# A fused attention and two-MLP kernel: due times shifted by twenty drawn tables, a warm-up of TensorE, tanh for SiLU in one chunk, and four smaller edits

## The chip, the cores and the metric

The kernel runs on one core of a Trainium2 chip. The metric is the device time of one execution, in microseconds (us); three runs of the kernel before gave 1001.65, 1002.58 and 1002.89, median 1002.58. Engines: PE is TensorE (matmuls), DVE is VectorE, ACT is ScalarE, POOL is GpSimd, and SP issues nearly all DMAs. Each engine works through its own list of instructions in a fixed order; semaphores tie the lists together.

## The reference

Three steps in a row, in float32. Attention with random features over 4 batches, 8 heads, 576 tokens and head size 64: `phi(x) = exp(proj - |x|^2/2 - max) / sqrt(128)` with `proj = x omega^T` and 128 features, then `num = phi(q) (phi(k)^T v)` and `den = phi(q) sum(phi(k)) + 1e-6`, and their quotient. The heads side by side make 2304 rows of 512 columns. Then two MLPs:

```
x = (silu(x @ w_gate) * (x @ w_val)) @ w_out      # 512 -> 1536 -> 512
x = ((x @ w_a) * (x @ w_b)) @ w_out2
```

## The kernel before, in words

All of it is one launch with the tokens along the free axis. The 2304 tokens are cut into five chunks of 512, 512, 256, 512 and 512 (`spans`). For each chunk, queries and keys of a pair of heads go through `features` (a projection on PE, its maximum on DVE, exponentials on ACT), and `own` or `shared` makes the attention output. Chunks 0, 1 and 2 then run `layer(c, m)` for m = 0 (SiLU) and m = 1 (no activation); the last two chunks are taken as a pair (`pair(m, ...)`). A matrix product in float32 is made of three products of rounded parts: every operand is split into a high part (a copy rounded to the engine's format, by ACT) and a low part (the difference, by DVE or POOL), and PE does high*high, high*low and low*high (L936 to L938 in `layer`). In a pair, blocks of 2x2 are multiplied by seven products instead of eight (`seven`, with the sums and differences of the blocks made by DVE and POOL in L1016; all its matmuls are L994); only the last third of the down projection of m = 0 is done with eight (`plain`).

In `layer`, an up block f makes two PSUM banks, gate and value; ACT takes SiLU of the first (L954), DVE multiplies by the second (L957), and the result is split (L960 and L478). The exponentials (L632) and SiLU need different activation tables, and ACT loads one when it changes between them (ACT_TABLE_LOAD). Weights come as 64-bit words in chunk 0 and, half of them, in chunk 1: two ACT and two DVE instructions (L896 to L905) make floats of them; they are kept in DRAM and loaded again later.

No order is written out by hand. Every operation is given to a planner (`Plan.add`) with its engine, a cost, what it reads and writes, and a due time. `Plan.order` plays the engines forward: an engine that is free takes, of the operations whose inputs are there by its costs, the one with the smallest due time; buffers of a ring are handed out in the order in which they were recorded. The order that results is the program. So a shift of due times moves instructions everywhere, and on all engines.

Places that the change touches: `constants` (L503 on: omega, the table warm-up, the identity that POOL makes), `loads` and `keys` (the transposed keys of the first pair of heads, one DMA of 288 KB), `layer` (L954 to L957), `mixes` (splits and differences that the pair needs at its start), `seven`, `down` and `plain` (the pair's products), and `issue`.

Of the kernel before, what the change touches and what calls it, by code (L numbers as in the profile page):

```python
# [96 lines left out]
class Plan:  # L97
# [14 lines left out]
    RATE = 0.24  # L112
    HELD = {DVE: (1.0, 0.05), POOL: (1.0, 0.12)}
# [28 lines left out]

# [121 lines left out]
    def issue(self):  # L264
        for o in self.order():
            o.fn()
# [3 lines left out]
def attention_moe_moe(ctx: ExitStack, tc: tile.TileContext, qT, kT, q, k, v, omegaT,  # L270
# [192 lines left out]
    def pe(t):  # L463
        return dict(pace=t, lat=t + 0.17)
# [23 lines left out]
    AHEAD = 20.0  # L488

# [13 lines left out]
    def constants():  # L503
# [29 lines left out]
    def features(rT, tok, nt, step, f, due, length, how, psum, first):  # L533
# [39 lines left out]
        for g in range(0, nt, size):  # L573
# [25 lines left out]
            else:  # L599
                ps = psum.buf()  # L600
                for i in range(n):
                    def proj(i=i, ps=ps, g=g):
# [10 lines left out]
                       [(rT, *rT.state), (bd, *bd.state)], writes=[(ps, i)])  # L613
# [24 lines left out]
    def loads(rT, src, p, due, pieces):  # L638

        for b, a, z, to in pieces:  # L640
            on(SP, dma((z - a) / 2), due - 9, lambda b=b, a=a, z=z, to=to: nc.sync.dma_start(
                out=rT.tile[:, to:to + z - a], in_=src[b, p][:, a:z]), writes=[(rT, b)])
# [3 lines left out]
    def keys(b, p, due, length, how):  # L646

        rT, tok, vt = r_xT.buf(), r_kt.buf(), r_vt.buf()
        loads(rT, kT, p, due, [(b, 0, S, 0)])
# [275 lines left out]
    def layer(c, m):  # L925
# [16 lines left out]
        for f in range(NF):  # L942
# [4 lines left out]
            for g in range(2):  # L947
# [6 lines left out]
            on(ACT, act(n, 0, True), due, lambda a=a, ps=ps: nc.scalar.activation(  # L954
                out=a.tile[:, 0:n], in_=ps[0].tile[:, 0:n], func=AF.Silu if m == 0 else AF.Copy),
                reads=[(ps[0],)], writes=[(a,)], table="silu" if m == 0 else None)
            on(DVE, dve(n), due, lambda a=a, h=h, ps=ps: nc.vector.tensor_tensor(  # L957
                out=h.tile[:, 0:n], in0=a.tile[:, 0:n], in1=ps[1].tile[:, 0:n], op=ALU.mult),
                reads=[(a,), (ps[1],)], writes=[(h,)])
# [59 lines left out]
    def mixes(m, due, eng):  # L1019
# [6 lines left out]
        def keep(name, k, b):  # L1026
            hi, lo = r_cx.buf(), r_cx.buf()
            got[name, k] = (hi, lo)
            split(of(b), of(hi), of(lo), due)

        def first(k):
            keep("a11", k, x[0, k])
            s3 = r_tmp.buf()
            combine(eng[k], of(x[0, k]), of(x[1, k]), of(s3), ALU.subtract, due)
            keep("s3", k, s3)
            less.append(s3)
# [51 lines left out]
    def pair(m, eng):  # L1088
# [23 lines left out]
        def seven(w, x, late, read):  # L1112


            b0, b1, b2 = (ps_m.buf() for _ in range(3))
            b4, b3 = (b2, b1) if late else (b1, b2)
# [5 lines left out]
            for i, name in enumerate(order):  # L1122
                b, wn, xn, first, last = steps[name]
                product(b, w[wn], x[xn], now(6 * i), first, last)
                read(name, b)

        def up(f, late):
# [18 lines left out]
            seven(w, x, late, read)  # L1146
# [9 lines left out]
        def down(g, d, hx):  # L1156

            w = mixed_weights(m, 2 * NF + ND * d + g, 2 * NF + ND * (d + KD // 2) + g, now(), d == 0)
            e = now(42) - 15
# [5 lines left out]
            seven(w, hx, d == 0, read)  # L1165

        def plain(g, d, hx, more):
# [4 lines left out]
            for t, names in ((1, ("a21", "a22")), (0, ("a11", "a12"))):  # L1172
                for x, o in zip(i, (d, d + KD // 2)):
                    b = ps_m.buf()
                    hi, lo = parts_of[c, m, x]
                    for k, name in enumerate(names):
                        product(b, [(hi, lo, slice((2 * k + e) * P, (2 * k + e + 1) * P))
                                    for e in range(2)], hx[name], now(more), k == 0, k == 1)
                        more += 6
                    gain(b, (t, o), now(more) - 15)  # L1180
# [43 lines left out]
        for f, out in steps:  # L1224
# [6 lines left out]
            else:  # L1231
                down(*out, hx[out[0]])
                done += n_down // (KD // 2)
        for (t, d), o in sorted(acc.items()):
# [80 lines left out]
```

## Time and profile before

| | |
|---|---|
| median of 3 runs | 1002.58 us (1001.65 to 1002.89) |
| profiled execution | 1005.29 us |
| its span, first to last instruction | 1003.5 us |
| PE busy | 984.2 us, 98% of the span |
| DVE busy | 894.3 us, 89% |
| ACT busy | 725.3 us, 72% |
| POOL busy | 258.2 us, 26% |
| granted TensorE clock, mean | 0.998 |

The profiled execution lies 1.8 us above its own span and 2.7 us above the median of the runs. [...] Waits are listed by who waited and who ended the wait.

### The profile page before, as it was taken

How to read it: one execution, taken by the hardware profiler on the slowest of the kernel's cores; microseconds unless marked ns; L12 is line 12 of the kernel's file. 1: busy time of each engine (PE TensorE's matmuls, PEld its weight loads, DVE VectorE, ACT ScalarE, POOL GpSimd, SP SyncE). 2: the span in 40 equal slices, each digit the busy share in tenths (PEclk: the TensorE clock that was granted, in tenths of full speed). 3: DMA queues.
4: the chain of work that ended last, by engine and by line, in shares of the span. 5: the costliest groups of instructions: out<-in, count | busy, mean ns of one | idle time of the engine just before them, and what ended most of it. 6: DMA issues, size and time to landing. Idle time of an engine off the chain costs nothing.

```text
span 1003.5 us, 15362 instructions
## 1 busy us (share of the span) xinstructions
PE 984.2 (98%) x5144; PEld 829.3 (83%) x5144; DVE 894.3 (89%) x1593; ACT 725.3 (72%) x1523; POOL 258.2 (26%) x207
## 2 busy tenths in 40 slices
PE   7999999999999999999999999999999999999998
PEld 6878888878878888888888999988888887888886
DVE  5999889999968889998978879989889788989997
ACT  5978878798789898879868978666574645556351
POOL 1220023413502333454356424112020021202020
PEclk9999999999999999999999999999999999999999
DMA  8778776686876567665654555511212301121212
GB/s 250 238 258 243 229 244 200 217 252 189 286 227 197 176 190 241 203 188 166 192 165 131 147 160 172 171 61 33 74 43 63 95 22 53 32 74 42 61 35 84
DMA packets 92400, 153.12 MB, mean 153 GB/s; under 512 B 8736, under 2 KB 41120, under 8 KB 92320
## 3 DMA queue, kind: packets, MB, share of 16 engines
q1 hardware_dynamic: 92240, 152.11, 49.3%
q8 instruction: 40, 0.66, 0.3%
q14 instruction: 40, 0.33, 0.1%
q10 hardware_dynamic: 80, 0.03, 0.0%
HBM read 128.52 MB, written 23.59 MB: 152 GB/s over the span
## 4 chain that ended last, share of the span: by engine, by line
PE 78%; DVE 9%; ACT 6%; DMA 3%; issue 2%; POOL 1%; SPq 0%; DVEq 0%; ACTq 0%; POOLq 0%
PE ps_m L994 12%; PE ps_m L936 12%; PE ps_m L937 11%; PE ps_m L938 11%; PE ps_t L994 8%; PE ps_p L994 8%; PE ps_kv L994 4%; PE ps_kv L663 3%; PE ps_p L583 2%; DMA w64a<-w 1%; PE ps_t L869 1%; DVE wl L478 1%; PE ps_p L609 1%; PE ps_t L854 1%; DVE w L905 1%
## 5 line engine op out<-in xcount | busy, mean ns | idle before, releaser
L478 DVE TENSOR_TENSOR wl<-w,wh 128x512 fp32r<-128x512 f32 x254 | 190.8, 761 | 10.2 <-ACT wh L917 9.6
L936 PE MATMUL ps_m<-xh,wh 128*128 128x512 f32 (+1 forms) x504 | 189.2, 375 | 3.2 <-ACT a L954 2.5
L937 PE MATMUL ps_m<-xl,wh 128*128 128x512 f32 (+1 forms) x504 | 184.7, 366 | 0.7 <-DVE xl L478 0.7
L938 PE MATMUL ps_m<-xh,wl 128*128 128x512 f32 (+1 forms) x504 | 184.5, 366 | 0.7 <-DVE wl L478 0.7
L917 ACT ACTIVATE wh<-w 128x512 fp32r<-128x512 f32 x220 | 135.9, 632 | 32.1 <-DVE w L905 18.6
L478 POOL TENSOR_TENSOR rs<-xT,rs 64x576 fp32r<-64x576 f32 (+4 forms) x48 | 67.9, 1414 | 201.4 <-ACT rs L566 114.6
L936 PEld LDWEIGHTS ps_m<-xh,wh 128*128 128x128 f32 x504 | 95.9, 190 | 18.2 <-ACT a L954 3.8
L938 PEld LDWEIGHTS ps_m<-xh,wl 128*128 128x128 f32 x504 | 95.6, 190 | 16.8 <-DVE wl L478 1.2
L937 PEld LDWEIGHTS ps_m<-xl,wh 128*128 128x128 f32 x504 | 95.9, 190 | 13.7 <-DVE xl L478 1.3
L936 PE MATMUL ps_m<-hh,wh 128*128 128x512 f32 (+1 forms) x240 | 90.9, 379 | 0.0
L937 PE MATMUL ps_m<-hl,wh 128*128 128x512 f32 (+1 forms) x240 | 88.6, 369 | 0.0
L938 PE MATMUL ps_m<-hh,wl 128*128 128x512 f32 (+1 forms) x240 | 88.6, 369 | 0.0
L905 DVE SCALAR_TENSOR_TENSOR w<-w,w64a 128x512 uint32<-128x512 uint32 x90 | 69.9, 780 | 5.3 <-ACT w L896 5.2
L902 DVE SCALAR_TENSOR_TENSOR w64a<-w64a 128x512 uint32<-128x512 uint32 x90 | 69.0, 772 | 3.0 <-ACT w64a L899 2.9
L899 ACT ACTIVATE w64a<-w64a 128x512 uint32<-128x512 uint32 x90 | 60.9, 681 | 13.4 <-DMA w64a<-w 12.9
L896 ACT ACTIVATE w<-w64a 128x512 f32<-128x512 f32 x90 | 60.1, 675 | 0.6 <-DVE wl L478 0.6
L478 DVE TENSOR_TENSOR hl<-h,hh 128x512 fp32r<-128x512 f32 (+1 forms) x72 | 51.9, 722 | 1.6 <-ACT hh L960 1.4
L938 PEld LDWEIGHTS ps_m<-hh,wl 128*128 128x128 f32 x240 | 45.2, 189 | 8.0
L936 PEld LDWEIGHTS ps_m<-hh,wh 128*128 128x128 f32 x240 | 45.3, 189 | 7.6 <-issue 1.7
L960 ACT ACTIVATE hh<-h 128x512 fp32r<-128x512 f32 (+1 forms) x72 | 40.3, 561 | 15.3 <-DVE h L957 15.1
L937 PEld LDWEIGHTS ps_m<-hl,wh 128*128 128x128 f32 x240 | 45.4, 189 | 5.9
L825 POOL TENSOR_TENSOR xt<-qf,fT 128x512 f32<-128x512 f32 (+2 forms) x31 | 35.3, 1140 | 49.9 <-ACT qf L632 26.7
(850 smaller groups left out, 2635.4 us busy)
## 6 DMA issues: line engine op xcount, KB each, us to landing
w64a<-w SPq DMA_DIRECT2D x90, 512.0 KB, 4.3
w<-kept SPq DMA_DIRECT2D x180, 256.0 KB, 2.7
kept<-w SPq DMA_DIRECT2D x72, 256.0 KB, 5.0
w64b<-w SPq DMA_DIRECT2D x18, 512.0 KB, 4.7
kt<-k_t SPq DMA_DIRECT2D x16, 320.0 KB, 3.8
vt<-v_t SPq DMA_DIRECT2D x16, 320.0 KB, 4.4
xT<-kT SPq DMA_DIRECT2D x16, 288.0 KB, 3.8
qt<-q_t SPq DMA_DIRECT2D x16, 256.0 KB, 4.0
```

The lines of the kernel that those rows point to most:

```text
L478: eng.tensor_tensor(out=out, in0=a, in1=hi.bitcast(F32), op=ALU.subtract)
L825: nc.gpsimd.tensor_tensor(out=pr.tile.rearrange("p (t h m) -> p t h m", t=2, h=2)[lo_:hi_, i:i + m], in0=f.tile[lo_:hi_, g + i:g + i + m], ...
L896: on(ACT, act(CW + 50), due - ahead - 10, lambda: nc.scalar.activation(out=w.tile, in_=raw.tile[:, :, 1].bitcast(F32), func=AF.Abs, scale= ...
L899: on(ACT, act(CW + 50), due - ahead - 10, lambda: nc.scalar.activation(out=raw.tile[:, :, 0], in_=raw.tile[:, :, 0], func=AF.Copy, scale=0 ...
L902: on(DVE, dve(CW, True), due - ahead - 9, lambda: nc.vector.scalar_tensor_tensor(out=raw.tile[:, :, 0], in0=raw.tile[:, :, 1], scalar=0x80 ...
L905: on(DVE, dve(CW, True), due - ahead - 9, lambda: nc.vector.scalar_tensor_tensor(out=w.tile.bitcast(U32), in0=w.tile.bitcast(U32), scalar= ...
L917: on(ACT, act(CW), due - ahead - 7, lambda: nc.scalar.activation(out=hi.tile.rearrange("p a c -> p (a c)"), in_=w.tile, func=AF.Copy), rea ...
L936: nc.tensor.matmul(o, lhsT=hi.tile[:, wi], rhs=a, start=first, stop=False)
L937: nc.tensor.matmul(o, lhsT=hi.tile[:, wi], rhs=b, start=False, stop=False)
L938: nc.tensor.matmul(o, lhsT=lo.tile[:, wi], rhs=a, start=False, stop=last)
L960: on(ACT, act(n), due + 2, lambda h=h, hh=hh: nc.scalar.activation(out=hh.tile[:, 0:n], in_=h.tile[:, 0:n], func=AF.Copy), reads=[(h,)], w ...
L994: nc.tensor.matmul(ps.tile, lhsT=flat(a.tile)[:, k], rhs=b.tile, start=first and i == j == 0, stop=last and i == len(w) - 1 and j == 2, sk ...
```

## The change

Seven edits, all in what is given to the planner:

1. `shift` runs before the order is made: for each of 20 numbers it draws, with that number as seed, a shift of 0 for most operations and of a normal deviate (0.5, 1 or 2 us wide, for 3, 10 or 30% of them) for the rest, and adds it to the due time.
2. `constants` adds one PE operation: the identity times itself, 12 matmuls of 128x128, into a PSUM bank, as soon as POOL has made the identity.
3. The first transposed keys are loaded by two DMAs (240 and 336 columns), and a projection waits only for the columns that it reads.
4. In chunk 2, m = 0, SiLU is made with tanh: ACT takes tanh(g/2) (in the table that exponentials use), DVE makes (1 + tanh) * g, and a second DVE instruction 0.5 * that * value in the place of the product of before.
5. `mixes`: the splits and the difference of its first step are due 6 us earlier.
6. `seven` takes a PSUM bank when it starts one, no longer three at its beginning, and yields after each product, so that two of them can run interleaved. The two down products of the last third of m = 1 do: of the first, products 1 and 2, of the second, products 1 and 2, and then by turns. Their results are due earlier (40 us before their end, not 15).
7. `plain`, for its second half: the output blocks in another order, those first that the next layer's `mixes` needs first.

```diff
+    KEPT = (
+        100001, 100008, 100009, 100027, 100035, 100144, 100162, 100315, 100395, 100658,
...
+    def shift(self):
+        for k in self.KEPT:
+            rnd = random.Random(k)
+            size, share = (0.5, 1.0, 2.0)[k % 3], (0.03, 0.1, 0.3)[k // 3 % 3]
+            for o in self.ops:
+                x = rnd.gauss(0, size) if rnd.random() < share else 0.0
+                if o.due > -1e5:
+                    o.due += x
...
+        self.shift()
         for o in self.order():
...
+        idle = ps_t.buf()
+        def turn_over():
+            for _ in range(IDLE):
+                nc.tensor.matmul(idle.tile[:, 0:P], lhsT=ident.tile, rhs=ident.tile, start=True,
+                                 stop=True)
+        on(PE, pe(IDLE * 0.215), -1e6, turn_over, reads=[(ident,)], writes=[(idle,)])
...
+        part = TS + P
+        loads(rT, kT, p, due, [(b, 0, part, 0), (b, part, S, part)] if due < 4 else [(b, 0, S, 0)])
...
+            how = AF.Copy if m else AF.Tanh if c in TANH else AF.Silu
+            half = 0.5 if how == AF.Tanh else 1.0
...
+            if how == AF.Tanh:
+                on(DVE, dve(n), due, lambda a=a, ps=ps: nc.vector.scalar_tensor_tensor(
+                    out=a.tile[:, 0:n], in0=a.tile[:, 0:n], scalar=1.0, in1=ps[0].tile[:, 0:n],
+                    op0=ALU.add, op1=ALU.mult), reads=[(ps[0],)], writes=[(a,)])
+                on(DVE, dve(n), due, lambda a=a, h=h, ps=ps: nc.vector.scalar_tensor_tensor(
+                    out=h.tile[:, 0:n], in0=a.tile[:, 0:n], scalar=0.5, in1=ps[1].tile[:, 0:n],
+                    op0=ALU.mult, op1=ALU.mult), reads=[(a,), (ps[1],)], writes=[(h,)])
...
         def first(k):
-            keep("a11", k, x[0, k])
+            keep("a11", k, x[0, k], due - 6)
...
+                if first:
+                    banks[b] = ps_m.buf()
+                product(banks[b], w[wn], x[xn], now(6 * turn(i)), first, last)
+                read(name, banks[b])
+                yield
...
+            e = now(6 * turn(6) + 6) - (40 if g == ND - 1 else 15)
...
+            if d == KD // 2 - 1:
+                places = [(0, 0), (1, 0), (1, 1), (0, 1)]
...
+            elif out[1] == 0:
+                run(*(down(*out[:1], d, hx[-1], True, lambda i, d=d: (
+                    i + 2 * d if i < 2 else 2 * i + d)) for d in range(KD // 2)))
+                done += n_down
```

Counted over the program: PE has 12 more matmuls, DVE 12 more instructions (24 scalar_tensor_tensor of 128x256 in the place of 12 products), ACT 8 table loads fewer (14, before 22), SP one DMA more; POOL's number is the same. Three places show how the instructions move.

PE's list at the start of the program; `bd` is omega on a block diagonal, `xT` the transposed keys and queries, `ident` the identity. Before:

```order
L609 MATMUL ps_m_61<-bd_71,xT_75 128x256 x2
L609 MATMUL ps_m_62<-bd_71,xT_75 128x256 x2
L609 MATMUL ps_m_63<-bd_71,xT_75 128x256
L609 MATMUL ps_p_64<-bd_71,xT_76 128x256 x2
L609 MATMUL ps_p_65<-bd_71,xT_76 128x256 x2
L663 MATMUL ps_kv_68<-vt_83,kf_82 128x129 x4
L609 MATMUL ps_m_61<-bd_71,xT_77 128x256
```

And of the change:

```order
L542 MATMUL ps_t_66<-ident_70 128x128 x12
L635 MATMUL ps_m_61<-bd_71,xT_75 128x256 x2
L635 MATMUL ps_m_62<-bd_71,xT_75 128x256 x2
L635 MATMUL ps_m_63<-bd_71,xT_75 128x256
L635 MATMUL ps_p_64<-bd_71,xT_76 128x256 x2
L635 MATMUL ps_p_65<-bd_71,xT_76 128x256 x2
L691 MATMUL ps_kv_68<-vt_83,kf_82 128x129 x10
```

The twelve products of the identity stand ahead of the first projection; the first five projections follow in the order of before, and all ten key products now come ahead of the next pair's first projection.

ACT's list in chunk 2, m = 0, around the attention output `w64a` of one pair of heads (`a` is SiLU's or tanh's output, `wh` and `hh` high parts, `qf` features). Before:

```order
L960 ACTIVATE hh_137<-h_133 128x256
L917 ACTIVATE wh_172<-w_165 128x512
L700 ACTIVATE w64a__4811<-ps_t_67 128x512
L954 ACT_TABLE_LOAD
L954 ACTIVATE a_131<-ps_kv_68 128x256
L954 ACTIVATE a_130<-ps_m_61 128x256
L592 ACTIVATE qf_107<-ps_p_64 128x256
```

And of the change:

```order
L945 ACTIVATE wh_172<-w_163 128x512
L999 ACTIVATE hh_138<-h_134 128x256
L728 ACTIVATE w64a__4821<-ps_t_67 128x512
L984 ACTIVATE a_131<-ps_m_62 128x256
L945 ACTIVATE wh_173<-w_164 128x512
L999 ACTIVATE hh_139<-h_132 128x256
L984 ACTIVATE a_130<-ps_m_63 128x256
```

No table is loaded there, and the two activations that stood behind one load stand apart, with a high part of a weight and one of `h` between them.

PE's list near the end of the program, in the two down products of the last third of m = 1; a bank starts with `hl_156` in the first product, and the weights' number tells the product. Before, the second down product's first step and what follows it:

```order
L994 MATMUL ps_kv_68<-hl_156,wh_167 128x512
L994 MATMUL ps_kv_68<-hh_145,wh_167 128x512
L994 MATMUL ps_kv_68<-hl_156,wl_174 128x512
L994 MATMUL ps_kv_68<-kvs__6587,wh_167 128x512
L994 MATMUL ps_kv_68<-hl_149,wh_167 128x512
L994 MATMUL ps_kv_68<-kvs__6587,wl_174 128x512
L994 MATMUL ps_m_61<-hh_146,wh_173 128x512
L994 MATMUL ps_m_61<-zb__6568,wh_173 128x512
L994 MATMUL ps_m_61<-hh_146,wl_180 128x512
L994 MATMUL ps_m_61<-hh_138,wh_173 128x512
L994 MATMUL ps_m_61<-hh_139,wh_173 128x512
L994 MATMUL ps_m_61<-hh_138,wl_180 128x512
```

And of the change, behind that first step (which writes `ps_p_64`):

```order
L1033 MATMUL ps_m_63<-hl_157,wh_173 128x512
L1033 MATMUL ps_m_63<-hl_158,wh_173 128x512
L1033 MATMUL ps_m_63<-hl_157,wl_180 128x512
L1033 MATMUL ps_m_63<-hl_151,wh_173 128x512
L1033 MATMUL ps_m_63<-fT__6551,wh_173 128x512
L1033 MATMUL ps_m_63<-hl_151,wl_180 128x512
L1033 MATMUL ps_p_65<-hl_153,wh_167 128x512
L1033 MATMUL ps_p_65<-kvs__6616,wh_167 128x512
L1033 MATMUL ps_p_65<-hl_153,wl_174 128x512
L1033 MATMUL ps_p_65<-hl_149,wh_167 128x512
L1033 MATMUL ps_p_65<-hh_139,wh_167 128x512
L1033 MATMUL ps_p_65<-hl_149,wl_174 128x512
```

The second down product's second step (six matmuls, of operands that are ready early) now stands between its first step and the first step that reads a block of the last up product (`hh_138` and `hh_139` before, `hl_149` and `hh_139` now).

## Rows read from the trace of the kernel before

**Rows 1.** The page, busy time by engine: us, share of the span, instructions.

```profile
PE 984.2 (98%) x5144; PEld 829.3 (83%) x5144; DVE 894.3 (89%) x1593; ACT 725.3 (72%) x1523; POOL 258.2 (26%) x207
```

**Rows 2.** Waits of PE, whole span: waiter <- releaser: us, times, longest.

```profile
PE ps_m L609 <- DMA xT<-kT: 4.7, 1, 4.7
PE ps_m L936 <- ACT a L954: 2.5, 3, 1.1
PE ps_kv L936 <- ACT a L954: 1.8, 1, 1.8
```

**Rows 3.** Windows: stretch, length, busy of PE, PEld, DVE, ACT, POOL, PEclk, DMA.

```profile
25.00:56.00 31.00, 29.09 (x191) 24.91 (x190) 28.61 (x76) 28.79 (x80) 6.42 (x9) 1.00 0.81 254
832.00:956.00 124.00, 124.00 (x548) 102.43 (x547) 115.87 (x202) 64.22 (x117) 17.29 (x11) 1.00 0.18 51
```

**Rows 4.** Timeline of PE, first 12 us: start, us, line, count, idle before.

```profile
4.65 4.60 PE L609 MATMUL ps_m<-bd,xT 128*128 128x256 f32 x10 [4.65 <-DMA xT<-kT]
9.42 2.04 PE L609 MATMUL ps_p<-bd,xT 128*128 128x256 f32 x8 [0.16 <-DMA xT<-qT]
```

**Rows 5.** Timeline of POOL, DVE and ACT, first 12 us.

```profile
1.01 0.29 POOL masks.py:199 TENSOR_SCALAR_AFFINE_SELECT ident<-ident 128x128 f32<-128x128 f32 x1
...
9.77 0.41 DVE L619 TENSOR_REDUCE bias<-ps_m 128x2 f32<-128x256 f32 x1
...
10.57 1.15 ACT L632 ACTIVATE kf<-ps_m,bias 128x128 f32<-128x128 f32 x4 [3.48 <-DVE bias L626]
```

**Rows 6.** Timeline of PE and DVE, 54 to 56 us, before PE runs full.

```profile
55.04 0.50 PE L936 MATMUL ps_m<-xh,wh 128*128 128x512 f32 x1 [0.69 <-ACT xh L705]
...
54.38 0.68 DVE L902 SCALAR_TENSOR_TENSOR w64b<-w64b 128x512 uint32<-128x512 uint32 x1
```

**Rows 7.** Timeline of PE, chunk 0: a single wait.

```profile
201.81 0.51 PE L938 MATMUL ps_m<-xh,wl 128*128 128x512 f32 x1 [0.72 <-DVE wl L478]
```

**Rows 8.** Timeline of ACT and PE in chunk 2, m = 0.

```profile
545.58 1.28 ACT L954 ACT_TABLE_LOAD   x1
546.88 0.39 ACT L954 ACTIVATE a<-ps_kv 128x256 f32<-128x256 f32 x1
547.32 0.39 PE L936 MATMUL ps_kv<-xh,wh 128*128 128x256 f32 x1 [1.84 <-ACT a L954]
567.59 0.39 PE L936 MATMUL ps_m<-xh,wh 128*128 128x256 f32 x1 [1.07 <-ACT a L954]
```

**Rows 9.** Windows before, over and within chunk 2, m = 0.

```profile
500.00:531.00 31.00, 31.00 (x176) 26.21 (x175) 22.44 (x40) 22.92 (x55) 16.63 (x15) 1.00 0.52 171
531.00:576.00 45.00, 42.09 (x331) 40.07 (x330) 40.59 (x79) 40.43 (x92) 22.09 (x17) 0.96 0.47 135
546.00:561.00 15.00, 13.69 (x96) 12.74 (x97) 13.59 (x26) 12.14 (x27) 6.54 (x5) 0.89 0.42 129
```

**Rows 10.** Groups by line and shape: the product of chunk 2.

```profile
L957 DVE TENSOR_TENSOR h<-a,ps_m 128x256 f32<-128x256 f32 x12 | 4.8, 408 | 0.7 <-PE ps_m L938 0.6
```

**Rows 11.** Timeline of PE where the pair's m = 0 ends and m = 1 begins.

```profile
826.99 0.62 PE L994 MATMUL ps_p<-kf__5373,wh 128*128 128x512 f32 x2
827.45 0.39 PE L994 MATMUL ps_p<-kf__5373,wl 128*128 128x512 f32 x1
...
830.35 0.40 PE L994 MATMUL ps_p<-xT__5977,wh 128*128 128x512 f32 x1
```

**Rows 12.** Timeline of PE, DVE and POOL, 962 to 987 us.

```profile
983.16 0.39 PE L994 MATMUL ps_m<-hh,wl 128*128 128x512 f32 x1
986.33 0.39 PE L994 MATMUL ps_m<-hl,wh 128*128 128x512 f32 x1
...
962.80 1.67 DVE L478 TENSOR_TENSOR hl<-xt__5908,kvs__6587 128x512 fp32r<-128x512 f32 x1
984.19 0.68 DVE L478 TENSOR_TENSOR hh<-h__6579,hh 128x512 fp32r<-128x512 f32 x1
...
962.18 1.74 POOL L1016 TENSOR_TENSOR qt__5281<-xt__5908,a__6455 128x512 f32<-128x512 f32 x1 [26.05 <-DVE xt__5908 L1104]
```

More of the change, by code (lines that the diff above doesn't have):

```diff
@@ L1 @@
 import heapq
+import random
 from contextlib import ExitStack
@@ L488, in attention_moe_moe @@
     AHEAD = 20.0
+    TANH = (2,)
+    IDLE = 12
     def mm(n):
@@ L612, in features @@
                        reads=[(hi,), (lo,), (bdh,), (bdl,)] if how == SPLIT else
-                       [(rT, *rT.state), (bd, *bd.state)], writes=[(ps, i)])
+                       [(rT, *(x for x in rT.state if x == 0 or step * (g + i) + P > x)),
+                        (bd, *bd.state)], writes=[(ps, i)])
                 keys_of = [(ps, *range(n))]
@@ L953, in layer @@
             h_of.append((hh, hl))
[L954 to L959, printed above, removed]
+            how = AF.Copy if m else AF.Tanh if c in TANH else AF.Silu
+            half = 0.5 if how == AF.Tanh else 1.0
+            on(ACT, act(n, 0, True), due, lambda a=a, ps=ps, how=how, half=half: nc.scalar.activation(
+                out=a.tile[:, 0:n], in_=ps[0].tile[:, 0:n], func=how, scale=half),
+                reads=[(ps[0],)], writes=[(a,)],
+                table="silu" if how == AF.Silu else None)
+            if how == AF.Tanh:
[5 more added lines that the diff above has]
+                    op0=ALU.mult, op1=ALU.mult), reads=[(a,), (ps[1],)], writes=[(h,)])
+            else:
+                on(DVE, dve(n), due, lambda a=a, h=h, ps=ps: nc.vector.tensor_tensor(
+                    out=h.tile[:, 0:n], in0=a.tile[:, 0:n], in1=ps[1].tile[:, 0:n], op=ALU.mult),
+                    reads=[(a,), (ps[1],)], writes=[(h,)])
             on(ACT, act(n), due + 2, lambda h=h, hh=hh: nc.scalar.activation(
@@ L1024, in mixes, with keep @@
         got, less = {}, []
-        def keep(name, k, b):
+        def keep(name, k, b, due=due):
             hi, lo = r_cx.buf(), r_cx.buf()
@@ L1031, in first @@
         def first(k):
-            keep("a11", k, x[0, k])
+            keep("a11", k, x[0, k], due - 6)
             s3 = r_tmp.buf()
-            combine(eng[k], of(x[0, k]), of(x[1, k]), of(s3), ALU.subtract, due)
-            keep("s3", k, s3)
+            combine(eng[k], of(x[0, k]), of(x[1, k]), of(s3), ALU.subtract, due - 6)
+            keep("s3", k, s3, due - 6)
             less.append(s3)
@@ L1110, in gate, with seven @@
                     out=u.tile, in_=u.tile, func=AF.Silu), writes=[(u,)], table="silu")
-        def seven(w, x, late, read):
-            b0, b1, b2 = (ps_m.buf() for _ in range(3))
-            b4, b3 = (b2, b1) if late else (b1, b2)
+        def seven(w, x, late, read, turn=lambda i: i):
+            banks = {}
+            b0, b4, b3 = range(3)
             steps = {"p1": (b0, "b11", "a11", True, False), "p2": (b4, "b21", "a12", True, True),
@@ L1123, in seven, with run @@
                 b, wn, xn, first, last = steps[name]
-                product(b, w[wn], x[xn], now(6 * i), first, last)
-                read(name, b)
+                if first:
[3 more added lines that the diff above has]
+                yield
+        def run(*steps):
+            for x in steps:
+                next(x)
+                next(x)
+            for _ in zip(*steps):
+                pass
         def up(f, late):
@@ L1145, in read @@
                         gate(u, e)
-            seven(w, x, late, read)
+            run(seven(w, x, late, read))
             return u1, u3, u2
@@ L1154, in gain, with down @@
                 snap(b, acc[key], e)
-        def down(g, d, hx):
-            w = mixed_weights(m, 2 * NF + ND * d + g, 2 * NF + ND * (d + KD // 2) + g, now(), d == 0)
-            e = now(42) - 15
+        def down(g, d, hx, late, turn=lambda i: i):
+            w = mixed_weights(m, 2 * NF + ND * d + g, 2 * NF + ND * (d + KD // 2) + g,
+                              now(6 * turn(0)), late)
+            e = now(6 * turn(6) + 6) - (40 if g == ND - 1 else 15)
             def read(name, b):
@@ L1164, in read @@
                     gain(b, (t, d + i * KD // 2), e)
-            seven(w, hx, d == 0, read)
+            return seven(w, hx, late, read, turn)
         def plain(g, d, hx, more):
@@ L1171, in plain @@
                 weights(c, m, x, now(more))
[L1172 to L1180, printed above, removed]
+            places = [(t, j) for t in (1, 0) for j in range(2)]
+            if d == KD // 2 - 1:
+                places = [(0, 0), (1, 0), (1, 1), (0, 1)]
+            for t, j in places:
+                b = ps_m.buf()
+                hi, lo = parts_of[c, m, i[j]]
+                for k, name in enumerate(("a21", "a22") if t else ("a11", "a12")):
+                    product(b, [(hi, lo, slice((2 * k + e) * P, (2 * k + e + 1) * P))
+                                for e in range(2)], hx[name], now(more), k == 0, k == 1)
+                    more += 6
+                gain(b, (t, d + j * KD // 2), now(more) - 15)
         hx, rows_of = [{} for _ in range(ND)], [[] for _ in range(ND)]
@@ L1230, in pair @@
                 done += 12 * NG
-            else:
-                down(*out, hx[out[0]])
+            elif out[0] < ND - 1:
+                run(down(*out, hx[out[0]], out[1] == 0))
                 done += n_down // (KD // 2)
+            elif out[1] == 0:
+                run(*(down(*out[:1], d, hx[-1], True, lambda i, d=d: (
+                    i + 2 * d if i < 2 else 2 * i + d)) for d in range(KD // 2)))
+                done += n_down
         for (t, d), o in sorted(acc.items()):
```

5 lines of the change are left out of this document (3 added, 2 removed).

## The prediction

> **What bounds the kernel now.** I read the busy times first: PE works 984.2 us of a span of 1003.5 [rows 1]. Only some 20 us of the span hold no matmul at all, and 4.65 of these lie ahead of the first [rows 4]. So PE bounds the kernel, and a change that leaves its matmuls as they are can win only where PE waits, or runs at the lower clock. The list of PE's waits says where that is: 4.7 us for the first keys, and a few single waits of about 1 to 2 us for activations of line L954 [rows 2]. The windows come next: between 25 and 56 us PE lacks 1.9 us of 31, while ACT and DVE have 28.8 and 28.6 of work; in 124 us of the pair (832 to 956) PE lacks nothing, though DVE is at 115.9 [rows 3]. Then I went through the timeline and compared the distance of starts with 0.23 us, which a product of 512 columns takes when nothing is in its way (826.99 to 827.45 is two of them [rows 11]). Too long distances remain at the start, in some single waits of chunks 0 and 1, in chunk 2, where the pair goes from m = 0 to m = 1, and near the end. They are taken one by one. The profiled execution took 1005.29 us, 1.8 over its span and 2.7 over the median of 1002.58; I sum differences on it and subtract the same 2.7 at the end. What a measurement of this kernel can tell from no change is about 0.2%, 2 us.
>
> **1. The identity's products.** The identity is made at 1.01 + 0.29 = 1.3 us; PE stands until 4.65. Then five projections (10 records) take 4.60, 0.92 for one of 256 columns; from 9.42 eight records take 2.04, so a projection takes 0.51 [rows 4, 5]. [...] A product of 128 columns is half a slow projection at most, 0.46, so twelve last 5.5 us from about 1.4 and end at 6.9: 2.2 us later than the keys land. If the clock rises meanwhile, the five projections need 2.55 instead of 4.60 and end at 9.4, where they ended at 9.25. The first exponential waits for DVE's last maximum (9.77) and starts at 10.57 [rows 5], so nothing is won that ACT could use. I take 0. The ends: if the twelve run at the higher clock soon, PE is ready before the keys and the projections save up to 2.05; if the clock doesn't rise until the keys are done, they start 2.2 late: −2.1 to +2.2. The second DMA for the keys is one issue more on SP ahead of the other loads of the start; the first one is smaller and may land sooner. Both are within those ends.
>
> [...]
>
> **2. The start, to 56 us.** Here ACT and DVE set the pace [rows 3]. The last thing before PE runs full is the high and low part of x, behind a word of a weight (L902, 0.68 us) on DVE [rows 6]. In the new lists ACT and DVE each have one operation fewer ahead of it; one has a pace of some 0.6. I take −0.6. The idle of this stretch bounds what can be won (−1.9), and a later load or a wrong guess of the draw could cost as much as an operation or two on DVE: +1.4.
>
> **3. tanh in chunk 2.** Eight table loads of 1.28 go, from the one engine that PE waits for here: PE stood 1.84 us at 547.3, behind a load (545.58) and one activation, and 1.07 at 567.6 [rows 8]. The granted clock of 546 to 561 is 0.89 in the mean; 0.11 of 15 us is 1.65 lost at the lower clock, right behind the first wait [rows 9]. Together 4.6. Against it, DVE gets 12 instructions of 128x256; the product it now makes takes 0.41 [rows 10], and the first scalar_tensor_tensor, which reads one bank and one tile too, should take the same: 4.9 us. DVE has 40.6 of 45 us in this stage and 22.4 of the 31 before it [rows 9], so 4.4 of spare inside and 8.6 ahead, where the planner may put work that is due later. It just fits. ACT falls from 40.4 to 30.2. What is late next is DVE's chain of two instructions from bank to `h`, 0.41 longer per block, where a block behind a load waited 1.28 for it. I take −3.5; the ends are −4.6 (all gone) and +0.5 (DVE, full, delays PE by what doesn't fit).
>
> **4. From m = 0 to m = 1 of the pair.** Seven steps from 826.99 to 830.35 take 3.36 where 1.61 would do [rows 11]. They wait for the first splits of m = 1, made of the last output blocks of m = 0. The plain product now makes first the blocks from which these come, and the splits are due 6 us earlier. A block of the plain product is 12 matmuls, 2.7 us, so one place earlier is enough for a loss of 1.75. I take −1.5, between −1.75 and 0 (the splits still wait for the rest of DVE's list).
>
> **5. The end.** From 983.16 to 986.33 seven steps take 3.17, 1.58 too many, since PE waits for `hh`, which DVE makes at 984.19 [rows 12]. Six matmuls whose operands are ready (1.36 us) now stand ahead of that place, and DVE's list is short of nothing else. I take −1.3, between −1.6 and 0. Behind the last matmul nothing changes.
>
> **6. The order drawn anew, elsewhere.** The two other waits for L954 (2.5 − 1.07 = 1.4, rows 2) and one for `wl` of 0.7 [rows 7] stand in chunks 0 and 1, where every instruction may move: each of the twenty draws adds to a small share of the due times, about 2 us in all (the root of the sum of squares). I take −0.8; −2.1 if all go, +2 if as many come. In the stretches where PE lacks nothing [rows 3] a new order can only lose: +0.6, from 0 to +3.
>
> The sum: 0 − 0.6 − 3.5 − 1.5 − 1.3 − 0.8 + 0.6 = −7.1. The profiled time would be 998.2, and the median 1002.58 − 7.1 = 995.5.
>
> **The rivals.**
>
> *A: DVE takes ACT's place in chunk 2.* Its 40.6 + 4.9 = 45.5 us do not fit into 45, and no work is moved ahead. Then term 3 is between −0.6 and +0.5, say 0, and the time 995.5 + 3.5 = 999. For it speaks DVE's share of 90% [rows 9]; against it, that PE's two waits there ended with ACT [rows 8] and that 8.6 us are free just ahead.
>
> *B: the draw makes new waits; slower.* The place is the stretch of 832 to 956, where DVE has 8.1 us of spare in 124 [rows 3] and makes every operand. One DVE split took 1.67 instead of 0.68 while a POOL sum of 1.74 ran [rows 12]: 1.0 for a collision. If the drawn order puts an operation that PE needs behind such a pair, PE stops, and a stop like that of 547.3 costs 1.84 and then 1.65 at the lower clock [rows 8, 9], 3.5 together. Two such stops (7.0) eat the gain; three give 995.5 + 10.5 = 1006. Against it: the stretch holds 11 POOL operations [rows 3], and no stop there now. [...]
>
> *C: the gain is given back in small waits.* Terms 4 and 5 only move PE's wait to the next product that DVE isn't ready for, and chunk 2 gives half. Then −1.7 is left of term 3, −0.6 of term 2, and +1.5 come elsewhere: about 1002, the same.
>
> *D: the warm-up wins time.* The clock rises before the keys are there and the first exponential starts 2 us earlier; ACT, which sets the pace to 56 us, hands that on: 995.5 − 2.1 = 993.4. For it: 3.3 us of PE stand empty [rows 4]. Against: twelve products at the slow clock outlast the keys.
>
> **How the numbers follow.** The forecast has 0.60, A 0.15, B 0.08, C 0.09, D 0.08. The forecast, A and D are faster by over 0.2%: 0.83; C is the same, 0.09; B is slower, 0.08. The likeliest gives 995.5. Its own terms at better ends (3 at −4.6, 6 at −2.1, 2 at −1.9) with D reach 995.5 − 1.1 − 1.3 − 1.3 − 2.1 = 989.7, so the range begins at 990; above, A with one more small wait, 999 + 2, gives 1001. C's upper half and B stay outside, under 2 in 10.
>
> **What would show it.** Fourteen table loads instead of 22, and no wait or granted clock below 1.00 in the stage of chunk 2 (term 3); DVE's share there, near 100% (A); starts 0.23 apart across the two places of terms 4 and 5; the first exponential at about 10.5 and not at 8.5 (D) or 12.7; the first full run of layer matmuls 0.6 earlier; waits of PE over 1 us in stretches that have none now (B). I am wrong if the time is over 1000.6, or if it falls by this much while chunk 2 keeps its waits.

## The result, and the profile after

The changed kernel takes 992.59 us (median of 4 runs, 991.79 to 993.40) against 1002.74 (4 runs): the ratio is 0.9904, 95% interval 0.9889 to 0.9919, faster by 10.15 us. The forecast was 995.5, in a range of 990 to 1001. The profiled execution took 993.40 with a span of 991.6; between the two profiled executions the span fell by 11.9.

The page of the changed kernel, busy time by engine, as in [rows 1], and the groups of table loads (busy us, mean ns of one, idle before):

```profile
PE 981.2 (99%) x5168; PEld 831.8 (84%) x5168; DVE 896.3 (90%) x1605; ACT 713.4 (72%) x1515; POOL 261.3 (26%) x207
L984 ACT ACT_TABLE_LOAD x6 | 7.7, 1283 | 0.1
L659 ACT ACT_TABLE_LOAD x6 | 7.7, 1283 | 0.1
```

With the two loads outside these groups that makes 14, where there were 22. The prediction has all eight that went in chunk 2, but only six stood there. These are the groups of the kernel before between 500 and 600 us:

```profile
L954 ACT ACT_TABLE_LOAD x3 | 3.8, 1283 | 0.1
L632 ACT ACT_TABLE_LOAD x3 | 3.8, 1283 | 0.1
```

The changed kernel has none in that stretch. The other two went in chunk 1: between 280 and 370 us there are twelve before and ten now. The waits of PE over the whole span, against [rows 2] (us in total, times, longest):

```profile
PE ps_kv L691 <- issue: 1.9, 1, 1.9
PE ps_t L542 <- POOL vt L546: 1.4, 1, 1.4
PE ps_t L768 <- DVE xl L495: 1.1, 1, 1.1
PE ps_m L635 <- ACT kf L659: 0.8, 1, 0.8
PE ps_m L964 <- ACT xh L733: 0.7, 1, 0.7
PE ps_t L822 <- DVE xt L813: 0.4, 1, 0.4
PE ps_m L965 <- DVE xl L495: 0.2, 1, 0.2
```

That is the whole list, and all of it lies in the first 56 us. Before, the waits for `a` (L954) alone came to 4.3 us [rows 2], all behind that point. The windows of the changed kernel (columns as in [rows 3, 9]):

```profile
25.00:56.00 31.00, 28.56 (x192) 25.29 (x191) 29.48 (x77) 27.50 (x77) 7.42 (x8) 1.00 0.81 265
500.00:531.00 31.00, 31.00 (x189) 26.61 (x188) 22.98 (x40) 23.25 (x58) 18.18 (x16) 1.00 0.51 160
531.00:576.00 45.00, 45.00 (x365) 42.45 (x365) 43.49 (x95) 37.50 (x94) 22.00 (x16) 1.00 0.48 143
832.00:956.00 124.00, 123.93 (x547) 102.29 (x546) 116.27 (x205) 64.71 (x118) 17.66 (x11) 1.00 0.18 54
```

From 531 to 576, where PE lacked 2.9 us and had a granted clock of 0.96, it is now full (45.00) at a granted clock of 1.00. The start is where it was. PE's first matmuls (start, us, count) and ACT's first exponential, against [rows 4, 5]:

```profile
1.36 4.71 PE L542 MATMUL ps_t<-ident 128*128 128x128 f32 x24 [1.36 <-POOL vt L546]
5.91 2.32 PE L635 MATMUL ps_m<-bd,xT 128*128 128x256 f32 x10
8.07 1.89 PE L635 MATMUL ps_p<-bd,xT 128*128 128x256 f32 x8
...
10.10 0.89 ACT L659 ACTIVATE kf<-ps_m,bias 128x128 f32<-128x128 f32 x3 [3.25 <-DVE bias L653]
```

The five projections take 2.32 instead of 4.60, but start 1.3 later; the first exponential starts at 10.10 instead of 10.57. The layer's first matmul behind `xh` starts at 55.13 instead of 55.04 [rows 6], and then this execution loses time that the one of before didn't lose there:

```profile
55.13 0.51 PE L964 MATMUL ps_m<-xh,wh 128*128 128x512 f32 x1 [0.69 <-ACT xh L733]
55.85 0.51 PE L965 MATMUL ps_m<-xl,wh 128*128 128x512 f32 x1 [0.22 <-DVE xl L495]
56.20 0.53 PE L966 MATMUL ps_m<-xh,wl 128*128 128x512 f32 x1
56.53 0.63 PE L964 MATMUL ps_m<-xh,wh 128*128 128x512 f32 x1
56.95 0.63 PE L965 MATMUL ps_m<-xl,wh 128*128 128x512 f32 x1
...
59.84 0.39 PE L965 MATMUL ps_m<-xl,wh 128*128 128x512 f32 x1
```

Starts 0.43 apart instead of 0.23: TensorE's granted clock was 0.50 from 56.3 to 59.7, and 1.7 us went. At the two places in the pair where [rows 11, 12] show holes, the steps of 0.23 no longer break. The first is the start of m = 1, with the product that reads `xT__6009`, the one that waits when the transition is undone (below). The second is the second down product's first step that reads a block of the last up product:

```profile
818.41 0.61 PE L1033 MATMUL ps_t<-kf__5364,wh 128*128 128x512 f32 x2
818.86 0.39 PE L1033 MATMUL ps_t<-kf__5364,wl 128*128 128x512 f32 x1
...
820.90 0.39 PE L1033 MATMUL ps_p<-xh,wl 128*128 128x512 f32 x1
821.13 0.39 PE L1033 MATMUL ps_m<-xT__6009,wh 128*128 128x512 f32 x1
...
973.84 0.39 PE L1033 MATMUL ps_m<-hl,wl 128*128 128x512 f32 x1
974.06 0.39 PE L1033 MATMUL ps_p<-hl,wh 128*128 128x512 f32 x1
...
974.97 0.39 PE L1033 MATMUL ps_p<-hh,wh 128*128 128x512 f32 x1
```

From 818.41 to 821.13 there are twelve steps in 2.72 us, from 973.84 to 974.97 five in 1.13.

**Where the time went.** A single wait is a row; many small ones are not, and the record of a matmul outlasts the step to the next one (0.39 us against 0.23 in the rows above). So I took, for every two successive matmuls, the distance of their starts less the median distance of that pair of shapes over both kernels' traces, and summed it by stretch. The identity's products count wholly as lost; what stands ahead of the first matmul and behind the last start is in the first and last column. Us lost, from one execution each:

| kernel | to 62 | 62–300 | 300–520 | 520–580 | 580–820 | 820–960 | from 960 | sum |
|---|---|---|---|---|---|---|---|---|
| before | 20.2 | 8.1 | 9.6 | 7.2 | 1.2 | 1.8 | 5.9 | 54.0 |
| changed | 21.8 | 5.0 | 7.2 | 2.2 | 1.2 | 0.2 | 4.4 | 42.0 |
| six edits, no draw | 23.9 | 9.4 | 9.2 | 4.5 | 1.5 | −0.2 | 4.6 | 52.9 |
| edits 4 to 7, no draw | 20.1 | 6.7 | 8.9 | 2.8 | 1.2 | −0.2 | 4.5 | 44.0 |
| before, draws of its own | 21.6 | 4.9 | 6.6 | 4.5 | 1.2 | 0.3 | 6.1 | 45.2 |
| before, the change's draws | 22.7 | 8.1 | 6.7 | 5.9 | 1.2 | 1.6 | 6.2 | 52.4 |
| six edits, other draws | 20.3 | 13.3 | 6.9 | 3.7 | 1.4 | 0.7 | 6.0 | 52.3 |

The rest of each span is 949 to 950.4 us of matmuls, so the sums tell the kernels apart. From the first line to the second: 5.0 us in chunk 2, 5.5 in chunks 0 and 1 (3.1 of it up to 300 us), 1.6 at the transition, 1.5 at the end, and 1.6 given back at the start, which is the stretch at the lower clock. Of the 5.0, 1.7 is the stretch at the lower clock that this execution of the kernel before had in chunk 2 (0.50 from 548.9 to 552.3).

The largest hole of the kernel before between 62 and 520 us stands behind a table load of chunk 1 (the first two lines). In the changed kernel the draws moved the exponentials there: ten stand in one run behind one load (the third line), where before ten stood behind two loads, with a load for SiLU and one activation between them:

```profile
289.06 1.28 ACT L954 ACT_TABLE_LOAD   x1
291.01 0.50 PE L936 MATMUL ps_m<-xh,wh 128*128 128x512 f32 x1 [1.09 <-ACT a L954]
...
301.71 3.03 ACT L659 ACTIVATE kf<-kf,bias 128x128 f32<-128x128 f32 x10
```

What this pair of loads is worth by itself no run shows.

### The profile page after: what moved, and what is told of

The parts are those of the page before. It is cut to its first block, busy times and chain, and to the rows that moved or that the text cites. A ratio compares the mean times of both kernels' runs of the same rounds, so it can differ in the third digit from the quotient of the medians.

```text
span 991.6 us, 15393 instructions
## 1 busy us (share of the span) xinstructions
PE 981.2 (99%) x5168; PEld 831.8 (84%) x5168; DVE 896.3 (90%) x1605; ACT 713.4 (72%) x1515; POOL 261.3 (26%) x207
## 4 chain that ended last, share of the span: by engine, by line
PE 93%; DVE 4%; ACT 1%; issue 1%; POOL 0%; DVEq 0%; POOLq 0%
PE ps_m L964 15%; PE ps_m L965 15%; PE ps_m L966 15%; PE ps_m L1033 12%; PE ps_p L1033 8%; PE ps_t L1033 8%; PE ps_kv L1033 4%; PE ps_kv L691 3%; PE ps_p L609 2%; PE ps_p L635 2%; PE ps_t L897 1%; PE ps_t L882 1%; PE ps_kv L966 1%; PE ps_kv L964 1%; PE ps_kv L965 1%
## 5 line engine op out<-in xcount | busy, mean ns | idle before, releaser
L930 DVE SCALAR_TENSOR_TENSOR w64a<-w64a 128x512 uint32<-128x512 uint32 x90 | 71.0, 793 | 3.5 <-ACT w64a L927 3.5
L966 PEld LDWEIGHTS ps_m<-hh,wl 128*128 128x128 f32 x240 | 45.2, 189 | 8.1 <-DVE wl L495 0.2
L495 DVE TENSOR_TENSOR hl<-h,hh 128x512 fp32r<-128x512 f32 (+1 forms) x72 | 47.7, 663 | 2.3 <-ACT hh L999 2.1
```

What stands on the lines that cost most here:

```text
L495: eng.tensor_tensor(out=out, in0=a, in1=hi.bitcast(F32), op=ALU.subtract)
L930: on(DVE, dve(CW, True), due - ahead - 9, lambda: nc.vector.scalar_tensor_tensor(out=raw.tile[:, :, 0], in0=raw.tile[:, :, 1], scalar=0x80 ...
L966: nc.tensor.matmul(o, lhsT=lo.tile[:, wi], rhs=a, start=False, stop=last)
```

## The experiments

Each was timed in five rounds against the kernel before on the same chip; an interval is that of the ratio.

**The identity's products.** In `turn_over`:

```diff
-            for _ in range(IDLE):
+            for _ in range(0):
```

> Leaves out the twelve products of the identity (the planner still counts their time, so every other instruction keeps its place). My theory: the first projections start at about 4.65 us at the lower clock and end about 1.4 us later than in the changed kernel, the first exponential comes up to 0.5 later, and ACT and DVE absorb it by 56 us: 992.6, within 1. Rival (the warm-up is worth what the projections save): 994 to 995, and the first full run of layer matmuls 1 to 2 us later.

Measured: 992.99 us, 0.9908 (0.9893 to 0.9922), no different from the changed kernel. PE and ACT at the start:

```profile
4.17 4.61 PE L635 MATMUL ps_m<-bd,xT 128*128 128x256 f32 x10 [4.17 <-DMA xT<-kT]
...
10.48 0.88 ACT L659 ACTIVATE kf<-ps_m,bias 128x128 f32<-128x128 f32 x3 [4.20 <-DVE bias L653]
```

The slow projections are back, end at 8.8 instead of 8.2, and the exponential comes 0.38 later. The identity's products are worth nothing that can be measured. PE starts at 4.17 here and not at 4.65 as in the kernel before: in this execution the first part of the keys landed 0.5 us sooner.

**The table loads back.** The planner still counts tanh and two DVE instructions, so the order stays:

```diff
-                out=a.tile[:, 0:n], in_=ps[0].tile[:, 0:n], func=how, scale=half),
+                out=a.tile[:, 0:n], in_=ps[0].tile[:, 0:n],
+                func=AF.Silu if how == AF.Tanh else how),
...
-                on(DVE, dve(n), due, lambda a=a, ps=ps: nc.vector.scalar_tensor_tensor(
...
+                on(DVE, dve(n), due, lambda: None, reads=[(ps[0],)], writes=[(a,)])
```

> Chunk 2, m = 0, with SiLU's own table again and one DVE instruction fewer per block, every instruction otherwise in the changed kernel's order; the loads come back (22). Theory (the table loads are what PE waited for): PE waits in the stage of chunk 2 for activations, 3 to 6 us with the stretch at the lower clock: 996 to 998.5. Rival (the new order, not the loads, cured chunk 2): below 994.

Measured: 997.09 us, 0.9949 (0.9933 to 0.9964), 4.5 over the changed kernel. There are 20 loads, not 22: the six of chunk 2 are back, the two of chunk 1 are not, since the order is the new one. Matched matmul by matmul with the changed kernel's trace, PE is 0.34 late at 529 us and 2.72 late at 604: 2.4 lost in chunk 2. Its largest wait there is this one:

```profile
560.23 0.83 PE L609 MATMUL ps_p<-oms,rs 128*128 128x256 f32 x4 [0.74 <-DVE qf L621]
```

The order took the two long waits for SiLU away even with the loads; the loads' price shows in smaller ones. The profiled execution shows 2.4 of the 4.5. That is the price of the loads less what a DVE that is 12 instructions (4.9 us) lighter gave back. The runs lie in two groups: three of 995.80 to 996.12 at mean granted clocks of 0.998 and 0.999, and three of 998.05 to 998.66 at 0.997; the profiled one is of the first.

**tanh alone.** The kernel before with edit 4:

```diff
+    TANH = (2,)
...
+            how = AF.Copy if m else AF.Tanh if c in TANH else AF.Silu
```

> The kernel before with tanh in chunk 2 as the only edit, planned anew. Theory: minus 4.6, the two waits and the half-clock stretch: 998, and no wait at about 547 and 567. Rival A (DVE becomes the bound there): minus 0 to 1.5, with waits on DVE in the stage. If the new plan happens to open or close other waits in chunks 0 and 1, they are seen in the list of PE's waits.

Measured: 998.82 us, 0.9965 (0.9952 to 0.9977), 3.45 under the kernel before in the same rounds (1002.27), where the forecast's term is 3.5. There are 16 loads. The losses of 520 to 580 fall from 7.2 to 2.8; both waits are gone but for a hole of 0.5 at 559 us. Rival A is out for an order that the plain due times give.

**The margin of DVE in chunk 2.** The product is issued twice:

```diff
-lambda a=a, h=h, ps=ps: nc.vector.scalar_tensor_tensor(
+lambda a=a, h=h, ps=ps: [nc.vector.scalar_tensor_tensor(
...
-                    op0=ALU.mult, op1=ALU.mult), reads=[(a,), (ps[1],)], writes=[(h,)])
+                    op0=ALU.mult, op1=ALU.mult) for _ in range(2)], reads=[(a,), (ps[1],)], ...
```

> The changed kernel's order, with the second of the two DVE instructions of each block of chunk 2, m = 0, issued twice (it writes the same again): 12 more of 0.41, 4.9 us. By rival A of the prediction (DVE is full in that stage) PE waits and 3 to 5 us are lost: 996 to 997. By my forecast's count (DVE had 4.4 spare inside and 8.6 ahead, and the chain to the product grows by 0.41 a block): 0 to 2 us, 992.6 to 994.6.

Measured: 994.84 us, 0.9920 (0.9904 to 0.9936), 2.2 over the changed kernel. The window and the one wait of PE between 500 and 600 us:

```profile
531.00:576.00 45.00, 44.26 (x352) 40.97 (x350) 44.59 (x105) 34.85 (x86) 21.35 (x16) 1.00 0.44 130
...
PE ps_kv L964 <- DVE h L992: 0.6, 1, 0.6
```

DVE is at 44.6 of 45, and of 4.9 us more work PE loses 1.7 in this stretch (by the sums above, 3.9 against 2.2). The time is just above my range of 992.6 to 994.6 and under rival A's 996. So the changed kernel's 43.5 of 45 left little. That the planner moved work ahead, as the forecast counted, the windows hardly show: from 500 to 531 DVE went from 22.44 us [rows 9] to 22.98.

**No draw.** `issue` without `self.shift()`:

```diff
     def issue(self):
-        self.shift()
```

> The changed kernel without the shift of due times; the other six edits stay and the order is planned from the plain due times. Theory (the draws took the single waits of chunks 0 and 1, which came out as about 5 us between 75 and 525 where I had put 0.8): about 997.5, with the waits back in that stretch and nothing in chunk 2, at the transition or at the end. Rival (the six edits did it, and the draws are idle): 993.

Measured: 1003.18 us, 1.0014 (1.0003 to 1.0024): all of the gain is gone, against both lines that were expected. PE's waits between 62 and 980 us:

```profile
PE ps_m L963 <- ACT a L983: 2.1, 3, 1.2
PE ps_m L963 <- DVE a L988: 1.8, 2, 0.9
PE ps_m L965 <- DVE wl L494: 1.5, 2, 1.2
PE ps_m L964 <- DVE xl L494: 0.2, 1, 0.2
```

The transition and the end stay cured (table, −0.2 and 4.6), but waits came back in chunks 0 to 2, the new `DVE a` (tanh's first DVE instruction) among them, and the start is 3.3 us later (the first matmul behind `xh` at 58.40).

**Edits 4 to 7 alone.** From the kernel without a draw, edits 2 and 3 undone:

```diff
-        loads(rT, kT, p, due, [(b, 0, part, 0), (b, part, S, part)] if due < 4 else [(b, 0, S, 0)])
+        loads(rT, kT, p, due, [(b, 0, S, 0)])
...
-        on(PE, pe(IDLE * 0.215), -1e6, turn_over, reads=[(ident,)], writes=[(idle,)])
```

> The kernel before with edits 4 to 7 alone (tanh, earlier splits, interleaved end, plain order); no draw, no identity products, one load of the first keys. Theory (the three local gains hold in the undrawn plan: about 3.5 + 1.8 + 1.5, and what the six undrawn edits lost came from the start that edits 2 and 3 plan anew): 995 to 997. Rival (planning anew for any edit opens new waits in chunks 0 and 1): 999 to 1004.

Measured: 995.43 us, 0.9924 (0.9911 to 0.9937). Waits of PE between 62 and 980 us:

```profile
PE ps_m L956 <- ACT a L976: 1.5, 2, 1.1
PE ps_m L956 <- DVE h L984: 0.4, 1, 0.4
```

The theory held. Adding edits 2 and 3 to these four costs 7.8 us in an undrawn plan (1003.18 − 995.43): 3.8 at the start, 2.7 between 62 and 300 and 1.7 in chunk 2 by the table. In the drawn plan leaving out the identity's products changes nothing (first experiment), and with both edits the start there loses 21.8, of it 1.7 at the lower clock, against 20.1 here and 23.9 without a draw. So most of the cost is not the edits' own; it is the plan that they upset. Which of the two does it, no run shows.

**Other numbers.** Each of the twenty is 100000 higher:

```diff
-        100001, 100008, 100009, 100027, 100035, 100144, 100162, 100315, 100395, 100658,
+        200001, 200008, 200009, 200027, 200035, 200144, 200162, 200315, 200395, 200658,
...
```

> The changed kernel with twenty other numbers to draw from (each 100000 higher; the widths and shares are distributed alike). Theory (which numbers they are decides; a draw as such is no help): about 1003, as without a draw, give or take 3, with other single waits between 62 and 520 us. Rival (any scatter of due times loosens the plan): 992 to 995.

Measured: 1005.29 us, 1.0030 (1.0020 to 1.0040). PE's largest waits behind 62 us:

```profile
PE ps_m L966 <- DVE wl L495: 2.9, 4, 1.6
PE ps_t L1033 <- DVE raw L1143: 1.1, 1, 1.1
PE ps_m L964 <- ACT wh L945: 0.9, 1, 0.9
```

**The change's draws in the kernel before.** `shift`, its numbers and its call as in the change, nothing else:

```diff
     def issue(self):
+        self.shift()
```

> The kernel before with the twenty draws as the only edit. They were not made for its list of operations. Theory (the draws help only with the list that they belong to): 1003, between 1000 and 1007, with single waits at other places between 62 and 520. Rival (the draws are good by themselves): 997 or less.

Measured: 1006.09 us, 1.0038 (1.0024 to 1.0052). The draws that help the changed kernel's list of operations cost 3.7 us in this one (1006.09 − 1002.43).

**Draws of its own for the kernel before.**

```diff
+    KEPT = (100002, 100010, 100011, 100024, 100036, 100081, 100908, 101457, 101556, 101673,
+        102222, 102402, 102825, 106543, 106560, 108288, 108613, 110763)
...
+        self.shift()
```

> The kernel before with 18 draws of its own as the only edit; each was kept because the planner, which plays the engines forward, ends its plan earlier with it. Theory (a search fitted to the list of operations is worth much by itself, the other six edits the rest): 996 to 999, with fewer single waits between 62 and 520 us, while the losses at the transition (1.8) and the end (1.5) stay. Rival (draws help only together with the other edits, which make the room): 1001 to 1006, like the unfitted draws.

Measured: 998.24 us, 0.9950 (0.9938 to 0.9962). Fitted draws are worth 4.6 without any of the other edits. One thing was missed: it cured the transition too (0.3 in the table), while the end stays (6.1).

**The last two down products in a row.** `run` of one product at a time, and their results due as before:

```diff
-            e = now(6 * turn(6) + 6) - (40 if g == ND - 1 else 15)
+            e = now(6 * turn(6) + 6) - 15
...
-            elif out[0] < ND - 1:
+            else:
                 run(down(*out, hx[out[0]], out[1] == 0))
```

> The changed kernel with the last two down products one after the other again, due as before. Theory: the loss of 1.58 near the end comes back, 992.6 + 1.5 = 994.1, with one wait of PE for DVE about 16 us before the end and no difference ahead of it. Rival (the draw alone would have removed it): 992.6.

Measured: 996.91 us, 0.9941 (0.9925 to 0.9957). Of three waits, two are ahead of the place I named, some 21 us before the end, and one is 5 us before it:

```profile
971.70 0.39 PE L1033 MATMUL ps_p<-hl,wl 128*128 128x512 f32 x1
972.73 0.51 PE L1033 MATMUL ps_p<-hl,wh 128*128 128x512 f32 x1 [0.64 <-ACT hl L1043]
973.80 0.50 PE L1033 MATMUL ps_p<-hh,wh 128*128 128x512 f32 x1 [0.57 <-DVE hh L495]
...
988.95 0.74 PE L1033 MATMUL ps_m<-hl,bdl__6418 128*128 128x512 f32 x2 [0.79 <-DVE w64a__5837 L1143]
```

Matched with the changed kernel, PE is 0.13 late at 956 us and its last matmul ends 2.8 later: 2.7 lost there, more than the 1.5 expected. The last wait, 0.79 for a bank that DVE had not yet read (L1143), has no counterpart among the waits of the kernel before. The median shows 4.3.

**The transition undone.** The plain product's blocks and the first splits as before:

```diff
-            if d == KD // 2 - 1:
+            if False:
...
-            keep("a11", k, x[0, k], due - 6)
+            keep("a11", k, x[0, k], due)
```

> The changed kernel with the plain product's blocks in the old order and the first splits of the pair due as before. Theory: 1.7 comes back where m = 0 goes to m = 1: 994.3, with waits of PE for a split there. Rival (either is hidden by the drawn order): 992.6. Moved splits at the start of the pair, at about 580 us, can cost up to 1 more.

Measured: 996.66 us, 0.9933 (0.9918 to 0.9948). The hole is the one of [rows 11], with the same waits:

```profile
820.78 0.50 PE L1033 MATMUL ps_t<-xh,wh 128*128 128x512 f32 x1
821.51 0.50 PE L1033 MATMUL ps_t<-xl,wh 128*128 128x512 f32 x1 [0.23 <-DVE xl L495]
822.82 0.50 PE L1033 MATMUL ps_m<-xT__6009,wh 128*128 128x512 f32 x1 [0.58 <-ACT a__6474 L1139]
```

In the trace PE goes from 1.39 late at 780 us to 3.19 at 832: 1.8, as expected. The median lies 4.1 over the changed kernel's; the profiled execution has 1.4 of that in the start, with a stretch of 3.4 us at a granted clock of 0.50 from 13.3, and one from 57.7.

**More draws.** Nine numbers behind the twenty:

```diff
+        500005, 500059, 500553, 501445, 503056, 503280, 503973, 504658, 506251,
```

> The changed kernel with nine draws more behind its twenty, kept by the same rule. Theory (what is left lies in the first 62 us, which the planner moves least, and no wait is left behind them): 990.5 to 992.5, same or slightly faster. Rival (the plan is fitted past what the chip follows, and new waits come): 994 or more.

Measured: 995.21 us (992.74 to 996.04), 0.9914 (0.9899 to 0.9929): not told apart from the changed kernel's 0.9904. My range of 990.5 to 992.5 was missed and the median is in the rival's, but the trace shows none of the waits that it named: the profiled span is 991.0, and no wait of PE is listed behind the first 62 us. The profiled execution is the fastest of the five, though; what the others lost isn't seen. No version had a median under the changed kernel's.

## Why the prediction was right

For terms 3, 4 and 5 the mechanism was right; two terms of the sum were mis-sized, the start (1 and 2) and the order drawn anew (6), and for the second the mechanism was wrong too. The terms against the profiled executions:

| term | forecast | measured |
|---|---|---|
| 1 and 2, the start | −0.6 | +1.6, of it 1.7 at the lower clock |
| 3, tanh in chunk 2 | −3.5 | −5.0 |
| 4, the transition | −1.5 | −1.6 |
| 5, the end | −1.3 | −1.5 |
| 6, waits drawn anew | −0.8 | −5.5 (−3.1 and −2.4) |
| 7, new waits | +0.6 | 0 |
| sum | −7.1 | −12.0 |

The step that failed is the sixth. I took its size from listed waits, 2.1 us, and let some of them go. But the waits that have a row are not all that PE loses: it was busy for 984.2 of 1003.5 us, and yet 54.0 us of that span are lost by the sums above. Between 62 and 520 us five holes of more than a quarter of a us that are gone in the changed kernel make 3.8, and smaller ones the rest; the stretch gave 5.5, over twice my bound. (Planning anew for edits 4 to 7 without a draw has 2.1 of that, 17.7 to 15.6 in the table; the rest came with the draws.) And I treated the draw as a scatter around the plan of before. It is not: twenty other numbers cost 12.7 us against these (1005.29 − 992.59), the same numbers cost 3.7 in the kernel before, and numbers fitted to that kernel gain 4.6. With all six other edits in, the draw decides: without it they are worth nothing (1003.18). I had no chance for that. It is not the only way to the gain, since edits 4 to 7 without any draw have 7.4 of it.

That the time lies in the range is in part luck. Term 6 gave 3.4 us more than its better end (−2.1), and the range reached low enough because I had let the warm-up win 2.1 and the start 1.9, neither of which came: without the two the better ends sum to 993.1.

The count for chunk 2 was right in its parts: both waits and the lower clock went, 43.5 us of DVE work found room in 45, and no new wait came. One reading was wrong, that all eight loads which go stood there; six did. The sum used the waits and not the number of loads, so it doesn't hang on it. The price by undoing in the same order is smaller than the 5.0, 2.4 in the trace: 1.7 of the 5.0 is lower clock in one execution, DVE is lighter in the undone version, and the rest fits a new order that hides part of the loads.

The median of edits 4 to 7 alone, 7.4 under before (1002.82 − 995.43), lies near my sum of −7.1, since terms 3 to 5 are those that could be read from rows.

The identity's products came out as counted in their net (term 1), with the clock up before the projections (1.00 from 5.10 us, they start at 5.91) and nothing for ACT to use; the 0.6 us that term 2 counted at the start did not come, lower clock or not: the first layer matmul behind `xh` starts 0.1 later than before. Rival D's gain of 2.1 was 0.47 at the first exponential and nothing at 55 us.

The trace of the kernel before has a granted clock of 1.00 from 9.54 us and no entry ahead of that; the records of the projections start 0.43 apart up to 8.62 and 0.22 apart from 9.78. In the changed kernel's trace the first entry, 1.00, is at 5.10, and the records of the identity's products start 0.21 apart up to 4.93 and 0.11 apart from 5.13. In eight executions whose first matmul starts at 1.36 us (the changed kernel and seven of the experiments), the granted clock rose at 4.2 to 6.7 us. This rise is what term 1 and rival D reckon with; what sets its moment no run shows.

Rival B came true in other draws as far as it says that a draw can make the kernel slower: those of the numbers 100000 higher are slower than before, with stops of up to 1.6 us for `wl` and one of 1.1 for an accumulator of the pair. Most of it lies between 62 and 300 us (13.3 lost against 8.1), not in the stretch that I named, and no run shows that a collision of DVE and POOL made the stops. That version has 22 table loads, eight of them between 56 and 122 us, where the changed kernel has two; how much of the loss is theirs was not tried.

The median fell less than the span (10.15 against 11.9) because the two profiled executions stand differently to their medians: 2.55 over it before (1005.29 against 1002.74), 0.81 after. I had subtracted 2.7 from both.

What stays open: which instructions the draws turned in chunks 0 and 1 besides the two loads, and what each is worth; which of edits 2 and 3 upsets the undrawn plan; whether draws fitted to edits 4 to 7 alone would do better than all seven; and how much of the 4 us that undoing the end or the transition costs in the median, beyond the 2.7 and 1.8 of the trace, is lower clock.

## What to carry to other kernels

Where a planner makes the order from due times, an edit's value can't be told apart from the plan that it lands in: judge each edit in a plan searched for it, or against the plain plan, and hold one fixed while the other moves. The waits that have a row were less than what a stretch lost here (2.1 us of them, where 5.5 were won); sum the distances between starts as well, before bounding what an order can give. Here a warm-up of TensorE was worth nothing (992.99 us without it, 992.59 with it), since the engine behind it waited for another (ACT's first exponential 3.25 us for DVE); look at that engine first. And where an engine changes tables, count the loads by stage: a new order alone changes their number (14 to 22 over the versions that have tanh in chunk 2).

## What the runs showed of the hardware

Two waits of 0.69 and 0.22 us around 55 us were followed by 3.4 us at a granted clock of 0.50 in this changed kernel's execution and not in that of the kernel without the identity's products, in the same order of instructions. The profiled executions with the transition undone, with the end undone and with nine more draws have such a stretch behind 55 us too, those with the table loads back and with the product issued twice don't. One such stretch (1.7 us lost of 991.6) brings the mean granted clock of a run to 0.998; of the changed kernel's four runs one has 0.998, one 0.999 and two 1.000. So what a short wait costs seems to vary from run to run of one program. With the end undone, the six runs took 994.17 and 994.48 at mean granted clocks of 0.999 and 1.000, and 996.22, 997.60, 997.77 and 998.57 at 0.997 to 0.998; with the transition undone, 992.91 at 1.000, and 996.24 to 997.35 at 0.996 and 0.997, but 993.71 at 0.998. The clock doesn't tell all: with nine more draws, runs of 992.74 and 996.04 have the same 0.998. I had counted a stretch at the lower clock as part of one wait's price; it is a price that some executions pay.
